# The last batch's attention output made turned, in 512 columns, in place of rows

## Chip, core and metric

One core of one Trainium2 chip runs one program: linear attention, then two feed-forward blocks. The metric is device time in microseconds (us), the median of the runs. TensorE (PE) does matmuls into eight PSUM banks, VectorE (DVE) and ScalarE (ACT) read PSUM, GpSimd (POOL) works between SBUF tiles, and SyncE (SP) issues the DMAs. Every engine runs its own instructions in the order in which the program holds them; semaphores make one wait for another.

## Reference, cut to what matters

```python
# attention: batch 4, heads 8, sequence 576, head size D 64, features M 128
q_p, k_p = phi(q_s), phi(k_s)
kv = np.einsum('bhsm,bhsd->bhmd', k_p, v)
z = np.sum(k_p, axis=2)
num = np.einsum('bhsm,bhmd->bhsd', q_p, kv)
den = np.einsum('bhsm,bhm->bhs', q_p, z)[..., None] + 1e-06
x = num / den                      # 2304 tokens x 512
# first block: 512 -> 2048 -> 512
h = np.maximum(x @ w_in, 0.0); x = h * h @ w_out
# second block: rms norm, gate and value 512 -> 1536 -> 512
```

`phi` is an exponential of a projection, less its norm and its maximum. All is in fp32. Where the kernel wants fast matmuls on fp32 data it splits an operand in two fp32r parts, high and low, and adds three products (high by high, high by low, low by high).

## The kernel before

The sequence of each batch is cut into 512 tokens (128 partitions times R = 4 rows) and a rest of 64 (SR). The four batches' 512 tokens are four blocks of the first feed-forward, `moe1(0)` to `moe1(3)`; the rests of all four batches make a fifth, `moe1(REM)`. `moe1(j)` runs over 16 chunks of 128 hidden columns: `hpart(c)` (12 matmuls of 512 columns into a bank `h`, L845) and `ypart(c)` (12 into four banks `acc`, L875). Then `moe2` does the second block, twice two batches (L1081, L1142).

The attention of batch b + 1 is woven into the matmuls of `moe1(b)`. `attention(b)` takes the eight heads as four pairs. For a pair: features of k and q (L604, exponentials on ACT at L628), `kv2` (L671, L674: key features times values and a column of ones, into one bank `kvp`; L658 also turns the rest's q features there), then the output. That is, in the long form which the last two batches use:

- `trs` (L726): eight 128x128 transposes of the q features into two banks; `copy` takes them to `qt` (ACT or DVE).
- `mms` (L731, L735): the turned q features are the weights, and `kv` with its column z (65 columns) is what moves: eight fp32 matmuls, and two for the rest. The output lies in rows, each with its denominator beside it.
- `rows` (L703 to L707): on DVE, the denominators of four rows plus epsilon, their reciprocal (4 columns), and the quotient.
- `xtr` (L773, L763): the finished rows are turned back by four transposes of 128 columns and one of 64, and `split` (L403 on ACT, L394 on DVE) makes the high and low part of `x`, which `hpart` of `moe1(b + 1)` reads.

Past the first batch all this goes through the two banks `t`. A fp32 matmul of `mms` or `kv2` shows in the trace as two TensorE instructions.

The order of every engine's instructions is set when the kernel is built, by `Plan`: a list scheduler that walks a clock of its own with an assumed cost of each piece, and at each step takes the ready piece of the least `prio` whose buffers are free. The priorities of a pair are `pb` (the batch's base, plus 3.7 for each pair) plus some tenths of its step. What the planner put in order stays in that order on the chip, however long the pieces take there. Weights for `moe1` come from HBM through a ring of 8 buffers `wr`. Between these, DVE and ACT decode weights for the second block (`decode`, L432 to L446), off TensorE's path.

Of the kernel before, what the change touches and what calls it, by code (L numbers as in the profile page):

```python
# [247 lines left out]
def kernel(  # L248
# [23 lines left out]
    nc = tc.nc  # L272
# [28 lines left out]
    slots = {  # L301
# [5 lines left out]
    }  # L307
    plan = Plan(slots)
# [60 lines left out]
    def f32(t):  # L369
        return t.bitcast(F32)  # L370
# [11 lines left out]
    def pe(n, cnt, passes=1):  # L382
        return cnt * passes * max(0.109, 0.0133 + n / 2400.0)
# [151 lines left out]
    def attention(b):  # L535
        base = (b - 1) * float(C1) if b else -25.0
        step = 3.7 if b else 6.0
        lead = base - (6.0 if b else 3.95)
        full, long = b < FULL, b >= LONG
        rem_x = []  # L540
        ssr = Buf(["sm"])

# [19 lines left out]
        def rem_prep(pr0):  # L562
# [3 lines left out]
            row_norms(pr0, xr, ssr)  # L566
            dma(lead, lambda: vr_t[P - SR:], lambda: rest_v[b], 133120, w=[b_vr])

        def pair(hp):
            banks = ["t"] if b else ["t", "h", "acc"] if hp < 3 else ["t", "acc"]  # L570
            pb = base + hp * step
            h0 = 2 * hp
            bv = b_v[(b * HP + hp) % 2]
            vt = v_t[(b * HP + hp) % 2]
# [79 lines left out]
            qrt = Buf(["qr"])  # L654

            def qtr2(o):
                for h in range(2):
# [21 lines left out]
                    plan.add("PE", 0.224 * 5, pb + 3 * u + h * u, kv, [(pk, h * R), pr, bv, b_vr, b_vz], [(kvp, h)],  # L679
                             kv_free)  # L680
            if long:
                plan.add("PE", 0.224 * 10 + 0.27, pb + 4 * u, kv2, [pk, pr, bv, b_vr, b_vz, b_const], [kvp], kv_free,
                         pre=[qrt])
# [115 lines left out]
    def moe1(j):  # L799
# [172 lines left out]
    def read_units(c, pos, gates):  # L972
        return {nm: read_unit(c, nm, pos + {"g": 0.0, "v": 0.3, "s": 0.05, "o": 1.0}[nm[0]], gates) for nm in UNITS}
# [61 lines left out]
    def operands(j, rv, p0, cls, gates, room):  # L1035

        ops = {nm: [] for nm in ("B11", "T2", "B21", "T3", "T1", "T4", "B22")}
        for kk in range(2):
# [12 lines left out]
            minus(p + 0.05, t, b22, t, 512)  # L1051
            two("T2", t, p + 0.05)
            two("T3", b12, p + 0.1)
            two("B22", b22, p + 0.1)
            b21 = scaled(p + 0.1, j, kk + 2, rv[0], gates, room)
            minus(p + 0.1, t, b21, t, 512)
            gates = [plan.nodes[-1]]
            two("B21", b21, p + 0.1)
            two("T4", t, p + 0.1)
        return ops  # L1060

    def operands_rem(rv, p0, gates, room):
        ops = {"B1": [], "B2": [], "D": []}
        for kk in range(2):
# [254 lines left out]
```

## Time and profile before

| what | us |
|---|---|
| three runs, median (lowest to highest) | 1006.02 (1003.1 to 1006.41) |
| the profiled execution, its own time | 1006.28 |
| its span in the trace | 1004.5 |
| PE busy in the span | 989.2 |
| DVE busy | 712.2 |
| ACT busy | 525.6 |
| mean granted TensorE clock | 0.996 of full |

Between span and time lie 1.8 us. A busy PE is one with a matmul in its pipe; how long a group of matmuls takes is read better from its start to the start of the next group. The page's chain of work that ended last lies for 88% of the span on PE.

### The profile page before, as it was taken

What the parts mean: (1) busy time and instruction counts of PE and PEld (TensorE: products, weight loads), DVE (VectorE), ACT (ScalarE), POOL (GpSimd) and SP (SyncE); (2) the same over time, 40 slices, a digit from 0 to 9 for tenths busy, and PEclk for the clock granted to TensorE, in tenths of its full rate; (3) what the DMA queues carried; (4) which work ended last, traced back from release to release, by engine and by line L of the source; (5) the groups of instructions that cost most, each with busy time, mean ns of one, the idle gap of its engine ahead of it and who ended that gap; (6) DMA issues with size and microseconds to landing.
All of it is one profiled execution on the core that took longest, in us unless ns stands there. A gap on an engine that the chain in (4) does not pass through costs nothing.

```text
span 1004.5 us, 14617 instructions
## 1 busy us (share of the span) xinstructions
PE 989.2 (98%) x5140; PEld 838.4 (83%) x5140; DVE 712.2 (71%) x1374; ACT 525.6 (52%) x1097; POOL 122.3 (12%) x101
## 2 busy tenths in 40 slices
PE   8999999999999999999999999999998999999998
PEld 7888888888888888888789978888886888888887
DVE  5989998577658576655622879889797747576673
ACT  5878888545564555544534557654353444224220
POOL 0110132131110101100000302311043000000000
PEclk9999999999999999999999999999999999999999
DMA  7777888976667575678868435234243212212213
GB/s 244 255 243 251 280 263 307 303 256 228 242 216 260 188 247 185 226 255 286 281 216 267 146 106 162 80 116 137 75 123 108 83 53 63 74 31 79 71 32 104
DMA packets 74841, 179.36 MB, mean 179 GB/s; under 512 B 8848, under 2 KB 12048, under 8 KB 74768
## 3 DMA queue, kind: packets, MB, share of 16 engines
q1 hardware_dynamic: 74768, 178.43, 54.2%
q8 instruction: 40, 0.66, 0.3%
q14 instruction: 33, 0.27, 0.1%
HBM read 143.27 MB, written 35.13 MB: 178 GB/s over the span
## 4 chain that ended last, share of the span: by engine, by line
PE 88%; DVE 4%; DMA 4%; issue 1%; ACT 1%; POOL 1%; SPq 0%; ACTq 0%; POOLq 0%; DVEq 0%
PE acc L875 18%; PE h L845 18%; PE acc L1081 11%; PE t L1142 11%; PE h L1081 10%; PE t L1081 3%; PE t L731 3%; PE t L604 2%; PE t L601 2%; PE t L671 2%; DMA st<-y 2%; PE t L726 1%; PE h L1142 1%; DVE cc L1101 1%; DVE wq L394 1%
## 5 line engine op out<-in xcount | busy, mean ns | idle before, releaser
L875 PE MATMUL acc<-g,wr 128*128 128x512 f32 (+1 forms) x660 | 151.7, 374 | 0.7 <-DVE g L394 0.7
L845 PE MATMUL h<-x,wr 128*128 128x512 f32 x528 | 133.4, 396 | 0.0
L875 PEld LDWEIGHTS acc<-g,wr 128*128 128x128 f32 x660 | 113.6, 189 | 21.3 <-DVE g L394 1.5
L1142 PE MATMUL t<-wq,ub 128*128 128x512 f32 x462 | 114.5, 392 | 0.7 <-DVE oa L1150 0.7
L1081 PE MATMUL acc<-x,wq 128*128 128x512 f32 x321 | 111.5, 396 | 1.8 <-DVE f L894 1.8
L845 PEld LDWEIGHTS h<-x,wr 128*128 128x128 f32 x528 | 97.2, 188 | 19.2
L403 ACT CAST wq<-wq 128x512 fp32r<-128x512 f32 x108 | 66.3, 619 | 87.3 <-DMA wq<-w2d4g 14.8
L1142 PEld LDWEIGHTS t<-wq,ub 128*128 128x128 f32 x462 | 86.7, 189 | 20.6 <-DVE oa L1150 2.4
L394 DVE TENSOR_TENSOR g<-f,g 128x512 fp32r<-128x512 f32 (+1 forms) x67 | 46.4, 693 | 70.1 <-ACT f L515 58.8
L859 ACT ACTIVATE f<-h 128x512 f32<-128x512 f32 (+1 forms) x80 | 44.9, 562 | 92.4 <-PE h L845 86.1
L1081 PE MATMUL acc<-xa,wq 128*128 128x512 f32 x231 | 89.9, 396 | 3.1 <-ACT xa L403 3.1
L394 DVE TENSOR_TENSOR wq<-wq 128x512 fp32r<-128x512 f32 x99 | 74.1, 756 | 25.5 <-ACT wq L403 25.0
L1081 PE MATMUL h<-x,wq 128*128 128x512 f32 x255 | 81.0, 390 | 0.0
L1081 PEld LDWEIGHTS acc<-x,wq 128*128 128x128 f32 x321 | 61.1, 191 | 15.1 <-DVE f L894 2.3
L875 PE MATMUL acc<-g,wu 128*128 128x512 f32 (+1 forms) x300 | 70.7, 376 | 0.2 <-DVE g L394 0.2
L1081 PE MATMUL h<-xa,wq 128*128 128x512 f32 x201 | 69.3, 390 | 0.4 <-DVE xa L394 0.4
L628 ACT ACTIVATE p<-t,sm 128x128 f32<-128x128 f32 x216 | 60.0, 383 | 18.1 <-DVE sm L619 18.1
L1101 DVE TENSOR_TENSOR cc<-acc,cc 128x512 f32<-128x512 f32 x84 | 57.7, 686 | 14.8 <-PE acc L1081 13.8
L1150 DVE TENSOR_TENSOR oa<-t,oa 128x512 f32<-128x512 f32 x75 | 50.8, 686 | 23.1 <-PE t L1142 22.7
L845 PE MATMUL h<-x,wu 128*128 128x512 f32 x240 | 61.6, 398 | 0.0
L875 PEld LDWEIGHTS acc<-g,wu 128*128 128x128 f32 x300 | 51.5, 189 | 9.5 <-DVE g L394 0.8
L441 ACT ACTIVATE dw<-st 128x512 f32<-128x512 f32 x68 | 46.6, 696 | 22.8 <-DMA st<-in_w_out_dram 9.4
(245 smaller groups left out, 1818.8 us busy)
## 6 DMA issues: line engine op xcount, KB each, us to landing
wr<-w1d SPq DMA_DIRECT2D x88, 512.0 KB, 4.3
st<-in_w_out_dram SPq DMA_DIRECT2D x28, 512.0 KB, 4.7
w1d<-wr SPq DMA_DIRECT2D x22, 512.0 KB, 4.1
st<-in_w_in_dram SPq DMA_DIRECT2D x16, 512.0 KB, 4.5
st<-in_w_gate_dram SPq DMA_DIRECT2D x12, 512.0 KB, 5.9
st<-in_w_val_dram SPq DMA_DIRECT2D x12, 512.0 KB, 5.9
st<-y SPq DMA_DIRECT2D x23, 256.0 KB, 4.1
v<-in_v_r_dram SPq DMA_DIRECT2D x16, 260.0 KB, 3.2
```

Source lines behind the costliest of these rows:

```text
L394: return lambda: en.tensor_tensor(out=lo(), in0=src(), in1=f32(hi()), op=ALU.subtract)
L403: first = plan.add("ACT", act(n), prio, lambda: nc.scalar.copy(out=hi(), in_=src()), rd, [whi], after, pre=[blo] if blo is not bhi else [])
L441: lambda: nc.scalar.activation(out=out(), in_=hf(), func=AF.Abs, scale=65536.0), [(st, 1)], [w])
L628: nc.scalar.activation(out=pbuf.ap[:, j0 + i, :], in_=fp.ap[:, i, :], func=AF.Exp, bias=mx.ap[:, i:i + 1])
L731: nc.tensor.matmul(np.ap[:, r * D1:(r + 1) * D1], lhsT=qt.ap[:, r * P:(r + 1) * P], rhs=kvt[:, h, :], start=True, stop=True)
L845: nc.tensor.matmul(hb.ap[:, :n], lhsT=u.ap[:, wl, kk * P:(kk + 1) * P], rhs=xcols(j, xl, kk)(), start=(gi == 0 and ii == 0), stop=(gi == l ...
L859: lambda: nc.scalar.activation(out=rb.ap[:, :n], in_=hb.ap[:, :n], func=AF.Relu), [hb], [rb])
L875: nc.tensor.matmul(accs[e].ap[:, :n], lhsT=u.ap[:, w, es], rhs=x.ap[:, :n], start=(c == 0 and i == 0), stop=(c == C1 - 1 and i == 2))
L1081: nc.tensor.matmul(bank.ap[:, cols], lhsT=u.ap[:, wl, c0 + kk * P:c0 + (kk + 1) * P], rhs=x[kk][xl].ap[:, :cols.stop - cols.start], start= ...
L1101: lambda: nc.vector.tensor_tensor(out=out.ap, in0=bank.ap, in1=x.ap, op=ALU.add), [bank, x], [out])
L1142: nc.tensor.matmul(o.ap, lhsT=x[xl].ap[:, c0:c0 + P], rhs=us[f"o{i}"].ap[:, wl, :], start=i == n == 0, stop=i == 1 and n == 2)
L1150: lambda: nc.vector.tensor_tensor(out=oa.ap, in0=o.ap, in1=oa.ap, op=ALU.add), [o, oa], [oa])
```

## The change

It touches the last batch (`turn = b == B - 1`), the planner's inputs around it, and two numbers of buffers.

- `turned_pair` takes the place of `mms`, `rows` and `xtr` for the four pairs of batch 3. From `kvp` it makes a weight tile of 256 columns, in a high and a low part: for each head 64 columns of kv and 64 copies of z (`k_hi` on ACT, `k_lo` on DVE). The rest's turned q features are split as well. `rest` is then six fp32r matmuls of 64 columns, `mms` six of 512 columns with q's turned features as what moves; these are now split in two (ACT and DVE) where they were copied. The result is turned already: 64 partitions of numerators and 64 of denominators, the denominators 64 times alike.
- `quotient` divides: ACT brings denominators (plus epsilon) and numerators to the right halves of the partitions, 64 partitions by 512 columns four times (and by 64 columns four times for the rest), DVE takes the reciprocal of all 128x512 denominators in two halves and multiplies. The product is split from SBUF.
- The ring `wr` goes from 8 to 7 buffers and `xw` from 2 to 3. The pairs of batch 3 have `pb` lower by 1.0.
- `moe1(REM)`'s `hpart` comes after the last `hpart` of batch 3; loads for the norms and the units of `moe2`, and its scaled operands, wait for further nodes.

```diff
@@ turned_pair, new
+            plan.add("ACT", 0.4, p0, k_hi, [kvp], [(k2, 0)])
+            plan.add("DVE", 0.4, p0, k_lo, [kvp, (k2, 0)], [(k2, 1)])
...
+            split(pb + 5 * u, qr_, lambda: qrh.ap, lambda: qrl.ap, 2 * SR, [kvp], qrh, qrl, psum=True)
+            er = Buf(banks, view=lambda t: t[:, :2 * SR].rearrange("p (h n) -> p h n", h=2))
+            PARTS = ((0, 0), (0, 1), (1, 0))
+            def product(o, h, x):
+                for i, (wl, xl) in enumerate(PARTS):
+                    nc.tensor.matmul(o, lhsT=k2.ap[:, wl, h * P:(h + 1) * P], rhs=x[xl](), start=i == 0, stop=i == 2)
...
+            plan.add("PE", 6 * 0.06, pb + 5.5 * u, rest, [k2, qrh, qrl], [er])
+            qps = [Buf(banks), Buf(banks)]
...
+            plan.add("PE", 0.88, pb + 6 * u, trs, [pq, b_const], qps)
+            for h in range(2):
+                split(pb + 6.2 * u, lambda h=h: qps[h].ap, lambda h=h: qh[h].ap, lambda h=h: ql[h].ap, 512, [qps[h]],
+                      qh[h], ql[h], psum=True)
+            nps = [Buf(banks), Buf(banks)]
...
+            plan.add("PE", 6 * 0.2267, pb + 8 * u, mms, [k2, *qh, *ql], nps)
@@ quotient
+                    nc.scalar.activation(out=xf.ap[lo_, cs], in_=den[0](hi_), func=AF.Copy, bias=EPS_DEN)
+                    nc.scalar.activation(out=xf.ap[hi_, cs], in_=den[1](lo_), func=AF.Copy, bias=EPS_DEN)
...
+                    return lambda: nc.vector.reciprocal(out=xf.ap[:, c0:c1], in_=xf.ap[:, c0:c1])
...
+                    nc.scalar.copy(out=nm.ap[lo_, :n], in_=num[0](lo_))
+                    nc.scalar.copy(out=nm.ap[hi_, :n], in_=num[1](hi_))
...
+                         lambda: nc.vector.tensor_tensor(out=xf.ap[:, cs], in0=nm.ap[:, :n], in1=xf.ap[:, cs], op=ALU.mult),
...
@@ attention, pair, moe1, moe2
-        "xr": 4, "wu": 10, "wr": 8, "dw": 2,
+        "xr": 4, "wu": 10, "wr": 7, "dw": 2,
-            pb = base + hp * step
+            pb = base + hp * step - (1.0 if b == 3 else 0.0)
+                if turn:
+                    turned_pair(pb, u, b, hp, pq, kvp, qrt, banks)
+                    return
...
-                h_nodes[c] = plan.add("PE", pe(n, len(group)), base + c, mm, list(dict.fromkeys(wb + xb)), [hb])
+                h_nodes[c] = plan.add("PE", pe(n, len(group)), base + c, mm, list(dict.fromkeys(wb + xb)), [hb],
+                                      [h_all[B - 1, C1 - 1]] if j == REM else [])
...
-    sets = [read_units(c, E1 + (c - 1.0 if c else -7.0), []) for c in range(NC2)]
+    sets = [read_units(c, E1 + (c - 1.0 if c else -7.0), [rv.users[0] for rv in rv01]) for c in range(NC2)]
```

The place that the prediction turns on is the passage from `moe1(2)` to `moe1(3)`, where the fourth pair's `x` is first read. In the rows, `acc` are the output banks of `moe1`, `h` a hidden bank, `t` the attention's banks, `g` the hidden activations, `x` the attention's output; the numbers name buffers. On PE before, from the turning back of the fourth pair to the first chunk of `moe1(3)`:

```order
L773 MATMUL t_4999<-ident,xw_4954 128x128 x4
L763 MATMUL t_5000<-ident,xw_4954 128x64
L875 MATMUL acc_3819<-g_4899,wr_4539 128x512
...
L875 MATMUL acc_3838<-g_4899,wr_4539 128x512
L845 MATMUL h_5032<-x_4037,wr_4665 128x512
L845 MATMUL h_5032<-x_4355,wr_4665 128x512
L845 MATMUL h_5032<-x_4745,wr_4665 128x512
L845 MATMUL h_5032<-x_5001,wr_4665 128x512
```

Nine `acc` matmuls of batch 2 stand between the turning back and the chunk, and its fourth matmul is the first to read the fourth pair's `x` (`x_5001`). On PE now, the same stretch, from the last `acc` matmul of batch 2:

```order
L981 MATMUL acc_3835<-g_4925,wr_4580 128x512
L601 MATMUL t_5012<-qr_4971,xw_4993 128x64
...
L615 MATMUL t_5034<-ident,p_4912 128x128 x4
L615 MATMUL t_5035<-ident,p_4912 128x128 x4
L601 MATMUL t_5067<-qt_5049,xw_4993 128x512
...
L601 MATMUL t_5068<-qt_5055,xw_4993 128x512
L950 MATMUL h_5098<-x_4139,wr_4666 128x512
L950 MATMUL h_5098<-x_4510,wr_4666 128x512
L950 MATMUL h_5098<-x_4831,wr_4666 128x512
L950 MATMUL h_5098<-x_5094,wr_4666 128x512
```

The last `acc` matmul has moved ahead of the fourth pair's whole output: `rest`, `trs` and `mms` follow each other with no other matmul between them, and the chunk that reads `x_5094` comes straight behind. On DVE before, the fourth pair's rows and its split (`sm` are the denominators of four rows):

```order
L707 TENSOR_TENSOR xw_4954<-t_4952,sm_4977 128x4x64
L706 RECIPROCAL sm_4977<-sm_4977 64x2
L703 TENSOR_SCALAR sm_4977<-t_4953 128x4
L707 TENSOR_TENSOR xw_4954<-t_4952,sm_4977 64x128
L706 RECIPROCAL sm_4977<-sm_4977 128x4
L707 TENSOR_TENSOR xw_4954<-t_4953,sm_4977 128x4x64
...
L394 TENSOR_TENSOR x_5002<-t_4999,x_5001 128x512
L432 TENSOR_SCALAR st_5021<-st_5021 128x512
```

No decoding step stands between the quotients and the low part of `x`; the next one (`st_5021`) comes behind it. On DVE now, over the same stretch (`st`, `dw` belong to the decoding of the second block's weights, `ld` is the low part of q's turned features):

```order
L1000 COPY f_5009<-acc_3826 128x512
L432 TENSOR_SCALAR st_4986<-st_4986 128x512
...
L641 RECIPROCAL xw_5026<-xw_5026 128x64
...
L437 TENSOR_SCALAR st_4991<-st_4991 128x512
L394 TENSOR_TENSOR ld_5050<-t_5034,qt_5049 128x512
L446 SCALAR_TENSOR_TENSOR dw_5045<-dw_5045,st_4991 128x512
L394 TENSOR_TENSOR ld_5056<-t_5035,qt_5055 128x512
...
L641 RECIPROCAL xw_5026<-xw_5026 128x256 x2
L655 TENSOR_TENSOR xw_5026<-ld_5086,xw_5026 128x512
L394 TENSOR_TENSOR x_5095<-xw_5026,x_5094 128x512
```

Two decodings of four steps each (`st_4986`, `st_4991`) now stand ahead of and between the two low parts, and the two reciprocals of 256 columns ahead of the product.

## Rows read from the trace of the kernel before

**Rows 1.** The page: busy time, share of the span and instructions of each engine.

```profile
PE 989.2 (98%) x5140; PEld 838.4 (83%) x5140; DVE 712.2 (71%) x1374; ACT 525.6 (52%) x1097; POOL 122.3 (12%) x101
```

**Rows 2.** Whom PE waited for: total us, times, longest us.

```profile
PE acc L1081 <- ACT xa L403: 3.1, 1, 3.1
PE acc L1081 <- DVE f L894: 1.8, 1, 1.8
```

**Rows 3.** PE in order of time, fourth pair: start, us, line, out<-in, shape, count.

```profile
429.83 1.00 PE L731 MATMUL t<-kv,qt 128*128 128x65 f32 x8
430.76 0.45 PE L735 MATMUL t<-kv,qr 128*64 128x65 f32 x4
431.13 1.11 PE L731 MATMUL t<-kv,qt 128*128 128x65 f32 x8
432.05 2.10 PE L845 MATMUL h<-x,wr 128*128 128x512 f32 x8
...
434.68 0.60 PE L773 MATMUL t<-ident,xw 128*128 128x128 f32 x4
435.21 0.27 PE L763 MATMUL t<-ident,xw 64*128 64x64 f32 x1
435.41 2.33 PE L875 MATMUL acc<-g,wr 128*128 128x512 f32 x9
437.58 2.88 PE L845 MATMUL h<-x,wr 128*128 128x512 f32 x12
440.30 2.88 PE L875 MATMUL acc<-g,wr 128*128 128x512 f32 x12
```

**Rows 4.** PE in order of time, a little earlier: fp32r of 256 columns, and transposes.

```profile
417.05 0.28 PE L604 MATMUL t<-bd_hi,tt 128*128 128x256 f32 x1
417.17 0.28 PE L604 MATMUL t<-bd_lo,tt 128*128 128x256 f32 x1
...
426.64 1.03 PE L726 MATMUL t<-ident,p 128*128 128x128 f32 x8
427.44 1.64 PE L875 MATMUL acc<-g,wu 128*128 128x512 f32 x6
```

**Rows 5.** ACT in order of time, fourth pair; in brackets idle time and its releaser.

```profile
425.41 0.66 ACT L441 ACTIVATE dw<-st 128x512 f32<-128x512 f32 x1
425.98 0.25 ACT L509 COPY qr<-t 128x128 f32<-128x128 f32 x1
427.28 1.08 ACT L509 COPY qt<-t 128x512 f32<-128x512 f32 x2 [1.05 <-PE t L726]
...
435.52 0.21 ACT L403 CAST xr<-t 128x64 fp32r<-128x64 f32 x1
```

**Rows 6.** DVE in order of time, fourth pair.

```profile
426.71 0.42 DVE L432 TENSOR_SCALAR st<-st 128x512 uint32<-128x512 uint32 x1
427.05 0.68 DVE L446 SCALAR_TENSOR_TENSOR dw<-dw,st 128x512 uint32<-128x512 uint32 x1
427.65 0.74 DVE L437 TENSOR_SCALAR st<-st 128x512 uint16<-128x512 uint16 x1
428.18 0.46 DVE L443 TENSOR_SCALAR dw<-dw 128x512 f32<-128x512 f32 x1
...
436.22 0.68 DVE L394 TENSOR_TENSOR g<-f,g 128x512 fp32r<-128x512 f32 x1
436.82 0.68 DVE L394 TENSOR_TENSOR x<-t,x 128x512 fp32r<-128x512 f32 x1
```

**Rows 7.** DVE in order of time, the norms ahead of the second block.

```profile
549.57 4.98 DVE L1011 RECIPROCAL wq<-wq 128x256 f32<-128x256 f32 x3 [1.57 <-ACT wq L1007]
```

**Rows 8.** Stretches: length, busy us of each engine (instructions), granted clock, DMA.

```profile
580.00:583.30 3.30, 1.04 (x5) 0.52 (x4) 3.30 (x7) 1.65 (x3) 0.00 (x0) 1.00 0.31 81
583.30:587.20 3.90, 3.90 (x11) 3.06 (x12) 2.14 (x4) 2.66 (x4) 0.00 (x0) 0.59 0.23 71
...
425.00:450.00 25.00, 25.00 (x126) 20.82 (x127) 15.69 (x34) 10.43 (x20) 1.51 (x1) 1.00 0.69 242
```

More of the change, by code (lines that the diff above doesn't have):

```diff
@@ L538, in attention @@
         lead = base - (6.0 if b else 3.95)
-        full, long = b < FULL, b >= LONG
+        full, long, turn = b < FULL, b >= LONG, b == B - 1
         rem_x = []
@@ L567, in rem_prep, with turned_pair, at, k_hi @@
             dma(lead, lambda: vr_t[P - SR:], lambda: rest_v[b], 133120, w=[b_vr])
+        def turned_pair(pb, u, b, hp, pq, kvp, qrh, banks):
+            k2 = Buf(["xw"], view=lambda t: t.rearrange("p r n -> p (r n)")[:, :512].bitcast(F32R).rearrange(
+                "p (a n) -> p a n", a=2))
+            qrl = Buf(["qr"], view=lambda t: t.bitcast(F32R))
+            kv_ = lambda: kvp.ap[:, :2, :D]
+            z_ = lambda: kvp.ap[:, :2, D:D + 1].to_broadcast([P, 2, D])
+            def at(i, q):
+                return k2.ap[:, i, :].rearrange("p (q d) -> p q d", d=D)[:, q, :]
+            KV, Z = slice(0, 4, 3), slice(1, 3)
+            def k_hi():
+                nc.scalar.copy(out=at(0, KV), in_=kv_())
+                nc.scalar.copy(out=at(0, Z), in_=z_())
+            def k_lo():
+                nc.vector.tensor_tensor(out=at(1, KV), in0=kv_(), in1=f32(at(0, KV)), op=ALU.subtract)
+                nc.vector.tensor_tensor(out=at(1, Z), in0=z_(), in1=f32(at(0, Z)), op=ALU.subtract)
+            p0 = pb + 4.5 * u
+            plan.add("ACT", 0.4, p0, k_hi, [kvp], [(k2, 0)])
+            plan.add("DVE", 0.4, p0, k_lo, [kvp, (k2, 0)], [(k2, 1)])
+            qr_ = lambda: kvp.ap[:, 2, :].rearrange("p (h n) -> p h n", h=2)
+            split(pb + 5 * u, qr_, lambda: qrh.ap, lambda: qrl.ap, 2 * SR, [kvp], qrh, qrl, psum=True)
[4 more added lines that the diff above has]
+                    nc.tensor.matmul(o, lhsT=k2.ap[:, wl, h * P:(h + 1) * P], rhs=x[xl](), start=i == 0, stop=i == 2)
+            def rest():
+                for h in range(2):
+                    product(er.ap[:, h, :], h, [lambda h=h: qrh.ap[:, h, :], lambda h=h: qrl.ap[:, h, :]])
+            plan.add("PE", 6 * 0.06, pb + 5.5 * u, rest, [k2, qrh, qrl], [er])
+            qps = [Buf(banks), Buf(banks)]
+            qh = [Buf(["qt"], view=lambda t: t.bitcast(F32R)) for _ in range(2)]
+            ql = [Buf(["ld"], view=lambda t: t.rearrange("p h r d -> p (h r d)").bitcast(F32R)) for _ in range(2)]
+            def trs():
+                for h in range(2):
+                    for r in range(R):
+                        nc.tensor.transpose(qps[h].ap[:, r * P:(r + 1) * P], pq.ap[:, h * R + r, :], ident)
+            plan.add("PE", 0.88, pb + 6 * u, trs, [pq, b_const], qps)
+            for h in range(2):
+                split(pb + 6.2 * u, lambda h=h: qps[h].ap, lambda h=h: qh[h].ap, lambda h=h: ql[h].ap, 512, [qps[h]],
+                      qh[h], ql[h], psum=True)
+            nps = [Buf(banks), Buf(banks)]
+            def mms():
+                for h in range(2):
+                    product(nps[h].ap, h, [lambda h=h: qh[h].ap, lambda h=h: ql[h].ap])
+            plan.add("PE", 6 * 0.2267, pb + 8 * u, mms, [k2, *qh, *ql], nps)
+            xf = Buf(["xw"], view=lambda t: t.rearrange("p r n -> p (r n)"))
+            rest_c, main_c = slice(512, 512 + SR), slice(0, 512)
+            def quotient(p1, num, den, cs, rd):
+                lo_, hi_ = slice(0, D), slice(D, 2 * D)
+                n = cs.stop - cs.start
+                def dens():
+                    nc.scalar.activation(out=xf.ap[lo_, cs], in_=den[0](hi_), func=AF.Copy, bias=EPS_DEN)
+                    nc.scalar.activation(out=xf.ap[hi_, cs], in_=den[1](lo_), func=AF.Copy, bias=EPS_DEN)
+                def recip(c0, c1):
+                    return lambda: nc.vector.reciprocal(out=xf.ap[:, c0:c1], in_=xf.ap[:, c0:c1])
+                nm = Buf(["ld"], view=lambda t: t.rearrange("p h r d -> p (h r d)"))
+                def nums():
+                    nc.scalar.copy(out=nm.ap[lo_, :n], in_=num[0](lo_))
+                    nc.scalar.copy(out=nm.ap[hi_, :n], in_=num[1](hi_))
+                plan.add("ACT", 2 * act(n), p1, dens, rd, [(xf, cs.start)])
+                plan.add("ACT", 2 * act(n), p1, nums, rd, [nm])
+                for c0 in range(cs.start, cs.stop, 256):
+                    c1 = min(c0 + 256, cs.stop)
+                    plan.add("DVE", 0.1 + (c1 - c0) * 0.0064, p1, recip(c0, c1), [(xf, cs.start)], [(xf, cs.start)])
+                plan.add("DVE", Shared(dve(n)), p1,
+                         lambda: nc.vector.tensor_tensor(out=xf.ap[:, cs], in0=nm.ap[:, :n], in1=xf.ap[:, cs], op=ALU.mult),
+                         [nm, (xf, cs.start)], [(xf, cs.start)])
+            for hl in range(2):
+                b_x[b, hl, hp] = Buf(["x"])
+            xh, xl = b_x[b, 0, hp], b_x[b, 1, hp]
+            rh, rl = b_xr[0, hp // 2], b_xr[1, hp // 2]
+            cr = slice(b * SR, (b + 1) * SR)
+            ers = [lambda ps, h=h: er.ap[ps, h, :] for h in range(2)]
+            quotient(pb + 7 * u, ers, ers, rest_c, [er])
+            split(pb + 8.6 * u, lambda: xf.ap[:, rest_c], lambda: rh.ap[:, hp % 2, cr], lambda: rl.ap[:, hp % 2, cr], SR,
+                  [(xf, 512)], (rh, (b, hp)), (rl, (b, hp)))
+            ns = [lambda ps, h=h: nps[h].ap[ps, :] for h in range(2)]
+            quotient(pb + 8.5 * u, ns, ns, main_c, nps)
+            split(pb + 9.5 * u, lambda: xf.ap[:, main_c], lambda: xh.ap, lambda: xl.ap, 512, [(xf, 0)], xh, xl)
@@ L653, in pair @@
             kv_free = list(bkv.users)
-            qrt = Buf(["qr"])
+            qrt = Buf(["qr"], view=lambda t: t.bitcast(F32R)) if turn else Buf(["qr"])
             def qtr2(o):
@@ L681, in pair @@
             if long:
-                plan.add("PE", 0.224 * 10 + 0.27, pb + 4 * u, kv2, [pk, pr, bv, b_vr, b_vz, b_const], [kvp], kv_free,
-                         pre=[qrt])
+                plan.add("PE", 0.224 * 10 + 0.27, pb + 4 * u, kv2, [pk, pr, bv, b_vr, b_vz, b_const], [kvp],
+                         [] if turn else kv_free, pre=[qrt])
+                if turn:
+                    turned_pair(pb, u, b, hp, pq, kvp, qrt, banks)
+                    return
                 copy(pb + 6.2 * u, lambda: qrt.ap, lambda: kvp.ap[:, 2, :].rearrange("p (h n) -> p h n", h=2), 2 * SR,
@@ L1037, in operands @@
         ops = {nm: [] for nm in ("B11", "T2", "B21", "T3", "T1", "T4", "B22")}
+        gates = gates + [r.users[-1] for r in rv]
         for kk in range(2):
@@ L1063, in operands_rem @@
         ops = {"B1": [], "B2": [], "D": []}
+        gates = gates + rv.users[-1:]
         for kk in range(2):
@@ L1232 @@
     room = ["st", "dw"]
-    rv01 = [rms(j, E1 - 10.0, [h3[4 + 2 * j]], ["xa"], room, ["wq"]) for j in range(2)]
+    rv01 = [rms(j, E1 - 10.0, [h3[4 + 2 * j], *last[-2:]], ["xa"], room, ["wq"]) for j in range(2)]
     x01 = operands(0, rv01, E1 - 8.0, ["x", "xa"], [h3[9]], room)
```

2 rows, old and new, of the table slots are left out of this document.

## The prediction

> **What bounds the kernel now.** I read the page's busy times first: PE is busy 98% of the span, DVE 71%, ACT 52% [rows 1]. Then the list of what PE waited for: nine entries, of which the two longest are 3.1 and 1.8 us, both in the second block [rows 2], and none in the attention of the last batch. Then PE in order of time through the last batch's fourth pair: each group starts where the one ahead has issued its last matmul, and the first chunk of `moe1(3)` follows at 437.58 without a gap [rows 3]. So this stretch costs what PE's instructions take from start to start, and work on DVE and ACT costs nothing as long as its results come in time. From 425 to 450 DVE is busy 15.69 of 25 us and ACT 10.43 [rows 8]: they have room on the average. The reader should ask two things of the change: how much PE work goes, and whether what PE now needs of DVE and ACT still lies beside other matmuls.
>
> **PE work removed.** `mms` runs from 429.83 to 432.05, that is 2.22 us; `xtr` from 434.68 to 435.41, 0.73 us [rows 3]. Together 2.95 us a pair.
>
> **PE work added.** Six fp32r matmuls of 512 columns: twelve take 440.30 - 437.58 = 2.72 us [rows 3], so six take 1.36. Six of 64 columns (`rest`): the trace has no fp32r matmul so narrow. Above, 256 columns take 0.12 [rows 4], and a 65-column pass of `mms` 0.93 / 8 = 0.116, the rest's 0.37 / 4 = 0.093 [rows 3]. Below, half of a 128-column transpose of 0.80 / 8 = 0.10 [rows 4], 0.05. I take 0.10, since all narrow matmuls here lie at 0.09 to 0.12 whatever their columns: 0.6 us, between 0.3 and 0.7. Net 2.95 - 1.36 - 0.60 = 0.99 a pair (0.87 to 1.29), and for four pairs **-4.0 us** (-5.2 to -3.5). `kv2`, `trs` and the features stay.
>
> The Trainium skill (TensorE: Matmul & The Clock Gate, "Back-to-back issue gap") gives matmuls of up to 64 columns an issue gap of some 60 cycles, about 25 ns, when nothing else binds. By it the four `rest` groups would take an estimated 0.6 us in all, and the sum would be 1.8 us lower than by my 0.10; no narrow matmul of this trace comes near it, so the rows keep the price.
>
> **The other engines' work.** Per pair DVE loses the row quotients (some 1.9 us of small steps) and gains the low parts of kv and of two 512-column q tiles, two reciprocals of 256 columns, one of 64, and a product. A DVE step of 512 columns starts 0.6 us after the one ahead [rows 6]; three reciprocals of 256 took 4.98 us [rows 7], 1.66 each. That makes about 7 us in place of 2.7, +4.5 a pair, 18 in all. ACT gains four copies of 64 partitions by 512. The trace has no ACT step on 64 partitions; I price it as 128x512, 1.08 / 2 = 0.54 [rows 5], the row of the same width; half of it, for half of the elements, is the other bound. For the first three pairs I let this lie beside `moe1(2)`: in the order each has at least 3 us of matmuls between `trs` and `mms`, and `h` and `acc` chunks behind `mms`. What is left of DVE's room there is a third of a pair's time at most, and banks `t` are held longer, so later features can wait. I allow 0 to 4 us for that and take 1.0. The ring of 7, the moved loads and the gates I cost at nothing: PE waited for no `wr` load before, and its order in the second block is the same; if a gate made one load late there, the wait would look like the 3.1 of [rows 2].
>
> **The fourth pair stands open.** This is where the change costs. Before, nine `acc` matmuls (2.17 us from 435.41 to 437.58) lay over the cast of the fourth pair's `x` [rows 3]. Now the last `acc` matmul of batch 2 stands ahead of `rest`, and from there to the chunk that reads the fourth `x` PE has only `rest` (0.6), `trs` (0.8), `mms` (1.36) and three matmuls of the chunk (0.68): 3.44 us. Beside it runs a chain that must go its whole length. I walk it from T = 0 at the end of the last `acc` matmul, with 0.2 us for each handing over (transposes of a half issue until about 427.04, the copy starts at 427.28 [rows 4, 5]), ACT steps of 512 columns at 0.54, 64-column ones at 0.2 (0.21), a decoding step of ACT at 0.57 [rows 5], and on DVE L432 0.34, L446 0.60, L437 0.53, L443 0.5 [rows 6]:
>
> - ACT copies the last `acc` bank (0.2 to 0.75), decodes (to 1.35), takes the rest's two denominators and two numerators (to 2.1). Only then is the second bank free, so the second half of `trs` runs from 2.3 to 2.7.
> - ACT decodes again (to 2.7), casts q's two halves (to 3.25 and 3.8). DVE works through its order: `acc` copy (to 0.6), L432, L437, L443, the 64-column reciprocal (about 0.45), L446, L432, L443 (behind ACT), L437, to 4.5. Then the first low part (to 5.1), L446 (to 5.7), the second low part (to 6.3).
> - `mms`: the first three start at 5.35, the other three at 6.5 and end at 7.2.
> - ACT's denominators to 8.0, its numerators to 9.1. DVE's two reciprocals from 8.2 to 11.5, the product to 12.2, ACT's cast from 12.4 to 13.0.
> - PE's fourth matmul of the chunk starts at 13.2.
>
> So PE stands still 13.2 - 3.44 = **9.8 us**. If DVE had its decoding done in advance and ACT too, the same walk gives: `trs` done at 2.15, low parts at 3.7, `mms` at 4.6, denominators at 5.4, reciprocals at 8.9, cast at 10.3, PE at 10.4, a stall of 7.0. With half price for 64 partitions it is 6.2. I take 9.8: the loads of these weights run ahead in SP's order, but in DVE's order the two decodings come behind the `acc` copy, which itself waits for PE, so they can't be done early. A late load there would make it more, 2 us at most I guess from a decoding's four steps (1.97).
>
> **The clock.** After the idle time before 583.3, PE's granted clock was 0.59 of full for 3.9 us and was 1.00 before it [rows 8]; that is mostly the lower level, 1.2 GHz. It cost 3.9 x 0.41 = 1.6 us. The stall here is longer, so I add 1.6 behind it, and 0.3 for the last matmuls of `mms` inside it (none to 0.6).
>
> **Sum.** -4.0 + 9.8 + 1.6 + 0.3 + 1.0 = +8.7. Against the profiled execution's 1006.28 that is 1015.0; the median of the runs lies 0.26 lower, so **1014.7 us**. Bounds of the terms: -5.2 + 6.2 + 1.6 = +2.6 gives 1008.6; -3.5 + 9.8 + 2.0 + 1.6 + 0.6 + 4.0 = +14.5 gives 1020.5.
>
> **Rivals.**
> 1. The saving shows whole: the fourth pair's chain would have to be hidden, as it was. 1006.0 - 4.0 = 1002.0. For it: PE hardly waits anywhere now. Against it: no matmul stands in PE's order that could hide it, and the chain's reciprocals alone take 3.3. Chance 0.04.
> 2. The stall is short and something is given back: the lower bound of 7.0 plus 1.6 of clock, and the 1.8 wait at the second block's entry goes (with its 1.6 of clock), since loads and `acc` copies stand otherwise there: -4.0 + 8.6 - 3.4 = +1.2, about 1007.2, within 0.3%. Against it: PE's order at that entry and the number of DVE steps ahead of the last `acc` copy are as before. Chance 0.08.
> 3. DVE becomes the bound through `moe1(2)` too: with +4.5 us a pair its low parts of `g` come late for `acc`. If each pair's added work overran the room by 1.5 to 2 us, 6 to 8 us would come on top: 1021. It decides from the point at which DVE's idle share in that stretch goes to nothing; 63% busy speaks against it. Chance 0.10.
>
> **Chances.** The forecast 0.78. A measurement here can tell about 0.3% (3.0 us) from no change. Faster 0.04, within 0.08, slower 0.88. The forecast's own bounds are 1008.6 to 1020.5; I take the low end to 1007.0 so that rival 2 lies inside. Outside are rivals 1 and 3, 0.14.
>
> **What would show it.** After: `rest` and `mms` of a pair together near 2.0 us, no `xtr`. In the list of what PE waited for, a wait of `mms` for DVE's low parts (2 to 4 us) and one of `h` at the chunk for ACT's cast of `x` (4 to 6 us), and a granted clock well under 1 for about 4 us behind it. If PE's timeline goes through this passage without those two, the prediction is wrong, and so it is if the first three pairs show waits of more than 4 us together.

## The result

| kernel | runs | median (lowest to highest), us |
|---|---|---|
| before | 4 | 1006.21 (1003.1 to 1007.34) |
| after | 4 | 1016.62 (1013.0 to 1018.88) |

The ratio is 1.0108, with a 95% interval of 1.0084 to 1.0132: the change makes the kernel about 10 us slower. The forecast was 1014.7 in a range of 1007.0 to 1020.5. The profiled execution of after took 1013.0 us and is the fastest of its four; its span is 1011.2.

### The profile page after: what moved, and what is told of

It reads as the page before. It is cut to its first block, busy times and chain, and to the rows that moved or that the text cites. A ratio compares the mean times of both kernels' runs of the same rounds, so it can differ in the third digit from the quotient of the medians.

```text
span 1011.2 us, 14550 instructions
## 1 busy us (share of the span) xinstructions
PE 986.6 (98%) x5088; PEld 834.3 (83%) x5088; DVE 725.3 (72%) x1366; ACT 544.5 (54%) x1141; POOL 127.8 (13%) x105
## 4 chain that ended last, share of the span: by engine, by line
PE 88%; DVE 7%; ACT 2%; DMA 2%; issue 1%; SPq 0%; POOL 0%; DVEq 0%; POOLq 0%; ACTq 0%
PE h L950 19%; PE acc L981 18%; PE t L1250 11%; PE acc L1189 11%; PE h L1189 10%; PE t L1189 3%; PE t L706 2%; PE t L703 2%; PE t L836 2%; PE t L773 2%; PE h L1250 1%; DVE wq L394 1%; PE t L831 1%; DVE cc L1209 1%; DVE xw L641 1%
## 5 line engine op out<-in xcount | busy, mean ns | idle before, releaser
L981 PE MATMUL acc<-g,wr 128*128 128x512 f32 (+1 forms) x660 | 151.0, 373 | 0.6 <-DVE g L394 0.4
L950 PE MATMUL h<-x,wr 128*128 128x512 f32 x528 | 135.5, 400 | 4.2 <-ACT x L403 4.2
L981 PEld LDWEIGHTS acc<-g,wr 128*128 128x128 f32 x660 | 113.8, 189 | 21.3 <-DVE g L394 1.2
L950 PEld LDWEIGHTS h<-x,wr 128*128 128x128 f32 x528 | 98.7, 191 | 24.9 <-ACT x L403 5.0
L1189 PE MATMUL acc<-x,wq 128*128 128x512 f32 x321 | 110.5, 393 | 0.0
L1189 PE MATMUL acc<-xa,wq 128*128 128x512 f32 x231 | 89.0, 393 | 3.6 <-ACT xa L403 3.2
L1189 PE MATMUL h<-x,wq 128*128 128x512 f32 x255 | 81.6, 392 | 0.6 <-DVE x L394 0.6
L1189 PE MATMUL h<-xa,wq 128*128 128x512 f32 x201 | 69.9, 393 | 2.7 <-ACT xa L403 1.9
L1189 PEld LDWEIGHTS acc<-x,wq 128*128 128x128 f32 x321 | 61.1, 190 | 13.1 <-DVE cc L1209 0.4
L981 PE MATMUL acc<-g,wu 128*128 128x512 f32 (+1 forms) x300 | 70.2, 375 | 0.0
L1209 DVE TENSOR_TENSOR cc<-acc,cc 128x512 f32<-128x512 f32 x84 | 57.7, 687 | 13.9 <-PE acc L1189 11.3
L950 PE MATMUL h<-x,wu 128*128 128x512 f32 x240 | 61.6, 397 | 0.0
L981 PEld LDWEIGHTS acc<-g,wu 128*128 128x128 f32 x300 | 51.6, 189 | 8.9
L1189 PEld LDWEIGHTS h<-x,wq 128*128 128x128 f32 x255 | 47.6, 189 | 10.8 <-DVE x L394 1.0
```

What stands on the lines that cost most here:

```text
L981: nc.tensor.matmul(accs[e].ap[:, :n], lhsT=u.ap[:, w, es], rhs=x.ap[:, :n], start=(c == 0 and i == 0), stop=(c == C1 - 1 and i == 2))
L1189: nc.tensor.matmul(bank.ap[:, cols], lhsT=u.ap[:, wl, c0 + kk * P:c0 + (kk + 1) * P], rhs=x[kk][xl].ap[:, :cols.stop - cols.start], start= ...
L1209: lambda: nc.vector.tensor_tensor(out=out.ap, in0=bank.ap, in1=x.ap, op=ALU.add), [bank, x], [out])
```

## The profile after

Line numbers of the code behind `turned_pair` are about 105 higher than before: `hpart` is L950, `ypart` L981, the second block's products L1189; `rest` and `mms` share L601, `trs` is L615. The page's line of busy times answers [rows 1]:

```profile
PE 986.6 (98%) x5088; PEld 834.3 (83%) x5088; DVE 725.3 (72%) x1366; ACT 544.5 (54%) x1141; POOL 127.8 (13%) x105
```

PE is busy for 2.6 us less and the span is 6.7 us longer. The list of what PE waited for (total, times, longest; sorted by total, parts left out):

```profile
PE h L950 <- ACT x L403: 4.2, 1, 4.2
PE acc L1189 <- ACT xa L403: 3.2, 1, 3.2
PE t L601 <- DVE ld L394: 2.1, 2, 1.8
PE h L1189 <- ACT xa L403: 1.9, 1, 1.9
...
PE t L615 <- ACT ld L647: 1.1, 1, 1.1
...
PE h L1189 <- DVE xa L394: 0.8, 1, 0.8
PE h L1189 <- DVE x L394: 0.6, 1, 0.6
```

The second stands in [rows 2] too, with 3.1. The first, third and fifth of these lines have no like there; they are one place, the fourth pair. PE in order of time there, from the last `acc` matmuls of batch 2 on (start, us, line, operation, shape, count; in brackets idle time and its releaser):

```profile
429.30 2.35 PE L981 MATMUL acc<-g,wr 128*128 128x512 f32 x9
431.49 0.76 PE L601 MATMUL t<-qr,xw 128*128 128x64 f32 x6
432.08 0.66 PE L615 MATMUL t<-ident,p 128*128 128x128 f32 x4
433.83 0.66 PE L615 MATMUL t<-ident,p 128*128 128x128 f32 x4 [1.10 <-ACT ld L647]
436.33 0.50 PE L601 MATMUL t<-qt,xw 128*128 128x512 f32 x1 [1.84 <-DVE ld L394]
...
437.53 0.79 PE L601 MATMUL t<-qt,xw 128*128 128x512 f32 x1 [0.24 <-DVE ld L394]
...
438.98 1.48 PE L950 MATMUL h<-x,wr 128*128 128x512 f32 x3
444.70 3.73 PE L950 MATMUL h<-x,wr 128*128 128x512 f32 x9 [4.24 <-ACT x L403]
448.26 2.88 PE L950 MATMUL h<-x,wu 128*128 128x512 f32 x12
```

Before, the chunk of `moe1(3)` followed the pair without a gap [rows 3]. Now 16.77 us pass from the start of `rest` at 431.49 to the second chunk at 448.26, for work that takes 5.48 at full speed (the prediction's 3.44, and 2.04 for nine more matmuls). So the passage costs 11.3 us. The four bracketed waits add up to only 7.4 of it: most of the rest is slow matmuls in and behind the stall. The windows view gives the nine matmuls behind it (length, busy us by engine, granted clock):

```profile
444.70:448.26 3.56, 3.56 (x9) 2.88 (x10) 2.70 (x5) 0.53 (x1) 0.00 (x0) 0.57 0.00 0
```

DVE in the same stretch shows the chain and what stands in it:

```profile
431.61 0.42 DVE L432 TENSOR_SCALAR st<-st 128x512 uint32<-128x512 uint32 x1
432.06 0.75 DVE L437 TENSOR_SCALAR st<-st 128x512 uint16<-128x512 uint16 x1
...
436.20 0.68 DVE L446 SCALAR_TENSOR_TENSOR dw<-dw,st 128x512 uint32<-128x512 uint32 x1
436.79 0.68 DVE L394 TENSOR_TENSOR ld<-t,qt 128x512 fp32r<-128x512 f32 x1
...
439.84 3.36 DVE L641 RECIPROCAL xw<-xw 128x256 f32<-128x256 f32 x2 [0.71 <-ACT xw L638]
443.30 0.69 DVE L655 TENSOR_TENSOR xw<-ld,xw 128x512 f32<-128x512 f32 x1
```

Decoding (L432 to L446) comes ahead of q's low part, then two reciprocals take 3.36 us, and only then come the product and the cast for which `h` waits.

To place the rest I read three points in each kernel's timeline of PE: the first matmul of `mms` for the fourth pair of batch 1 (`kv` is what moves; long ahead of the changed pairs), the first matmul of the second block, and the end. The first stretch is free of what the start of the program happened to cost (the first point is at 167.68 before, at 165.61 after):

| kernel | first point to second block | second block |
|---|---|---|
| before | 408.7 | 428.1 |
| after | 415.1 (+6.4) | 430.5 (+2.4) |

Sum: 6.4 + 2.4 - 2.1 (the earlier first point) = 6.7, the difference of the spans. Over all traces of this document the first point lies between 164.5 and 167.8, turned pairs or not.

## The experiments

The same three points for every experiment, in us (each from its one profiled execution), with the ratio of its runs to those of the kernel before on the same chip. The profiled execution is not always a typical one: e11's took 1015.83 us and is the slowest of twelve with a median of 1007.96, e7's took 1018.28 and is the slowest of six with a median of 1014.63. Their stretches can't be compared with the others to a us.

| run | pairs turned | to second block | second block | ratio (95%) |
|---|---|---|---|---|
| e1_first_three | 1 to 3 | 411.4 | 428.6 | 1.0036 (1.0022 to 1.0051) |
| e3_sides_only | none | 408.6 | 430.7 | 1.0017 (1.0001 to 1.0033) |
| e4_earlier3 | all | 424.9 | 429.4 | 1.0200 (1.0170 to 1.0231) |
| e6_three_earlier3 | 1 to 3 | 420.2 | 427.9 | 1.0112 (1.0091 to 1.0134) |
| c_short_recip | all | 413.0 | 432.5 | 1.0096 (1.0074 to 1.0118) |
| e7_decode_yields | all | 415.9 | 435.3 | 1.0109 (1.0090 to 1.0128) |
| e8_rows_decode_yields | none | 416.2 | 425.5 | 1.0052 (1.0036 to 1.0068) |
| e9_rows_no_gates | none | 408.2 | 428.5 | 1.0003 (0.9990 to 1.0016) |
| e10_yield_42 | all | 404.3 | 431.0 | 0.9985 (0.9967 to 1.0003) |
| e11_yield_40 | all | 413.8 | 432.5 | 1.0033 (1.0013 to 1.0053) |
| e12_rows_yield_42 | none | 409.3 | 431.7 | 1.0038 (1.0023 to 1.0052) |
| e13_yield_41_ring8 | all | 403.4 | 432.3 | 0.9989 (0.9970 to 1.0007) |

Theory: the loss is the turned fourth pair's chain, which nothing covers. Rivals: turned pairs overload DVE wherever they stand; the edits beside them (ring, priorities, gates) make the loss; the late place alone does.

### Which part of the change: e3, e1

All pairs in rows, everything else kept:

```diff
-        full, long, turn = b < FULL, b >= LONG, b == B - 1
+        full, long, turn = b < FULL, b >= LONG, False
```

> All four pairs in rows as before; only the other edits stay (ring wr 7, three xw buffers, last batch's priorities earlier by 1.0, the added gates). Theory: these cost what the second block's entry lost in the changed kernel, 0 to 2.2 us, and no wait stands in the passage from moe1(2) to moe1(3): 1006 to 1008.5. Rival (the other edits, not the turned pairs, make the loss): 1013 or more.

1006.71 us. No wait in the passage; the first stretch is as before (408.6 against 408.7), the second block 2.6 longer. The other edits are not the loss: 1.0017 here, 1.0108 for the whole change.

Three pairs turned, the fourth in rows:

```diff
+            turn = b == B - 1 and hp < 3
             pb = base + hp * step - (1.0 if b == 3 else 0.0)
```

> Pairs one to three of the last batch are made turned, the fourth in rows as before; all other edits stay. In PE's order the fourth pair still stands last in batch 2: six acc matmuls between its trs and mms, nothing between mms and xtr, nothing between xtr and the first chunk of moe1(3). Theory (the loss is the length of the turned fourth pair's chain, where nothing covers it): the stall of 9.8 us and the 1.5 us of slow clock go, 3.0 us of PE work are saved, the rows' shorter chain (quotient about 2 us, cast 0.6) leaves 2 to 3 us of stall, and the second block's entry still costs some 2 more: 1006 - 3.0 + 2.5 + 2 = about 1008 (1005 to 1010). Rival (it is the late place alone that costs, whatever form the pair has): PE still waits over 7 us in the passage, 1013 or more. Rival (the turned form costs in all pairs): 1013 or more with no long wait in the passage.

1008.64 us, as the theory had it, but by other terms: the second block costs 0.5 more than before instead of some 2, and the stall is 4.7 us instead of 2 to 3 (PE's list of waits; here lines behind the edit are one higher):

```profile
PE t L879 <- DVE xw L813: 4.7, 1, 4.7
```

DVE's timeline says why. The quotient of the rows takes DVE steps of 0.14 to 0.42 us, but the planner put decoding between them:

```profile
433.65 0.74 DVE L437 TENSOR_SCALAR st<-st 128x512 uint16<-128x512 uint16 x1
434.17 0.47 DVE L443 TENSOR_SCALAR dw<-dw 128x512 f32<-128x512 f32 x1
434.54 0.16 DVE L809 TENSOR_SCALAR sm<-t 128x4 f32<-128x4 f32 x1
434.67 0.69 DVE L446 SCALAR_TENSOR_TENSOR dw<-dw,st 128x512 uint32<-128x512 uint32 x1
435.28 0.17 DVE L812 RECIPROCAL sm<-sm 128x4 f32<-128x4 f32 x1
...
437.91 0.42 DVE L813 TENSOR_TENSOR xw<-t,sm 128x256 f32<-128x256 f32 x1
```

So the late place costs in either form, and the turned form costs more there: 11.3 us in all, against 4.7 and 1.5 of slow clock (the twelve matmuls behind took 4.25 us, 439.80 to 444.05, in place of 2.72). So rows in that place lose 6.2, over half of the 11.3. Why the fourth pair stands so late here and not in e3, where acc and h matmuls stand between its steps, no run shows.

### What the stall consists of: c_short_recip

```diff
+                    c1 = c0 + 4 if hp == 3 else c1
                     return lambda: nc.vector.reciprocal(out=xf.ap[:, c0:c1], in_=xf.ap[:, c0:c1])
```

> The changed kernel, but the fourth pair's three reciprocals take only 4 columns each instead of 256, 256 and 64, so the rest of that pair's denominators stays undivided; the order of every engine stays. Theory (the stall is the chain, and the reciprocals are a part of it until something else in the chain is later): the two large reciprocals take some 0.3 us in place of 3.36, but ACT's second copy of numerators ends at 441.0, so the product can start at 441.2 instead of 443.3 and the fourth matmul of the chunk follows 11.1 us after the start of rest in place of 13.2: 2.1 us less, 1016.5 - 2.1 = about 1014.4. If the reciprocals alone set the end, it is 3.1 less (1013.4). Rival (the wait is for something outside the pair's chain): no change, 1016 to 1017.

From the start of `rest` to the fourth matmul of the chunk 10.8 us (433.88 to 444.68) in place of 13.2. DVE's rows show the end that was foreseen: behind the short reciprocals the product waits for ACT's numerators. The last two rows are PE's.

```profile
442.09 0.24 DVE L642 RECIPROCAL xw<-xw 128x4 f32<-128x4 f32 x2 [0.71 <-ACT xw L638]
443.29 0.69 DVE L656 TENSOR_TENSOR xw<-ld,xw 128x512 f32<-128x512 f32 x1 [0.95 <-ACT ld L648]
...
444.68 2.35 PE L951 MATMUL h<-x,wr 128*128 128x512 f32 x9 [1.97 <-ACT x L403]
446.87 2.89 PE L951 MATMUL h<-x,wu 128*128 128x512 f32 x12
```

The nine matmuls behind took 2.19 us at a granted clock of 1.00, after an idle time of 1.97 us in place of 4.24. The length of the idle time alone does not decide this: at the second block's entry before, matmuls behind a wait of 1.8 us [rows 2] ran at 0.59 [rows 8]. To the second block it is 2.1 shorter than after, not the whole 3.8 that the passage gained (last section): this execution has three waits elsewhere (0.35, 0.30 and 0.74 us) that after's has not. The whole times (1014.1, ratio 1.0096 against 1.0108) agree with a small gain but could not show it alone. So 3.1 us of reciprocals are worth 2.4 of stall; without them the chain is still 10.8 long. The fourth pair's denominators stay undivided in this kernel, so it serves only for this measurement.

### Covering the chain by an earlier pair: e4, e6

```diff
-            pb = base + hp * step - (1.0 if b == 3 else 0.0)
+            pb = base + hp * step - (3.0 if b == 3 else 0.0)
```

> All four pairs turned; the last batch's priorities are earlier by 3.0 in place of 1.0, which puts four h and twelve acc matmuls (3.6 us) between the fourth pair's trs and mms and twelve acc matmuls (2.7 us) between its mms and the first chunk of moe1(3). Theory (the chain is as long as before, the cover decides): of the 6.0 us from the end of mms to the cast of x 3.4 are covered, so PE waits 2.6 us there and little ahead of mms; the clock may still fall for 1.5. 1006 - 4.0 + 2.6 + 1.5 + 2 = about 1008 (1005 to 1010). Rival (DVE cannot keep up with the added work, wherever PE's matmuls stand): the waits move, the time stays at 1013 to 1019.

In the passage the theory holds: `mms` starts without a wait, and PE waits 3.4 us for `x` (forecast 2.6). But the time is 1025.84, because another hole opens 120 us earlier, ahead of `moe1(2)`:

```profile
PE t L878 <- ACT p L730: 8.1, 1, 8.1
PE h L950 <- ACT x L403: 3.4, 1, 3.4
```

Batch 3's first pair now stands between the last transposes of batch 2 and the matmuls that would have covered them. In DVE's queue the first of its statistics (L717) is done at 314.4, but the next (L721) stands behind a decoding step that waits 2.49 us for its load, and behind the rest of two decodings; ACT's exponentials and PE stand behind L721:

```profile
313.75 0.69 DVE L717 TENSOR_REDUCE sm<-t 128x4 f32<-128x512 f32 x1 [0.59 <-PE t L706]
316.93 0.43 DVE L432 TENSOR_SCALAR st<-st 128x512 uint32<-128x512 uint32 x1 [2.49 <-DMA st<-in_w_val_dram]
...
320.43 0.15 DVE L721 SCALAR_TENSOR_TENSOR sm<-sm,sm 128x4 f32<-128x4 f32 x1
```

The same with the fourth pair in rows:

> Pairs one to three turned, the fourth in rows, and the last batch's priorities earlier by 3.0: twelve h and twelve acc matmuls now stand between the fourth pair's mms and its xtr, and nine acc matmuls (with four h) behind it ahead of the chunk that reads it. Theory: no wait in the passage, 3.0 us of PE work saved, the second block's entry costs 0 to 2.2 more: 1003 to 1005.5. Rival (three turned pairs cost on DVE or at the banks t what they save on PE): 1006 or more, with waits of t, g or x in the passage.

1016.2 us, missed for the same reason: the same wait ahead of `moe1(2)` (8.0 us), none in the passage. Moving whole pairs earlier moves the hole.

### Covering it by decoding that yields: e7, e8

Both times decoding stood in front of a step that PE needed. Its priority `pos` is ahead of the pairs'; now it is put behind:

```diff
-            decode(pos, st, lambda: w.ap, w)
+            decode(max(pos, 54.0), st, lambda: w.ap, w)
```

(and likewise for the four `both_sbuf` steps of `make_halves`).

> All four pairs turned, and the second block's decoding steps (decode and the sums and differences of its halves) get a priority behind the last batch's attention instead of ahead of it. In the new order eight DVE steps of decoding no longer stand in the fourth pair's chain, and PE has a chunk of h and fifteen acc matmuls (6.1 us) between the fourth mms and moe1(3). Theory (the loss was the uncovered chain, lengthened by decoding ahead of hot steps): no long wait in the passage, PE's saving of 4.0 shows, the second block's entry still costs 0 to 2.5: 1006 - 4.0 + 1.5 = about 1003.5 (1002 to 1005). Rival (turned pairs overload DVE, which then is late elsewhere): 1008 or more with new waits for DVE in moe1(2). Rival (the decoded weights now come late for the second block): 1008 or more with waits for wq at its entry.

The passage is as the theory wants it: from `rest` to the first chunk of `moe1(3)` at 436.08 PE waits once, 0.66 us, and for `g`, not for the pair:

```profile
425.54 0.76 PE L601 MATMUL t<-qr,xw 128*128 128x64 f32 x6
...
428.99 2.91 PE L950 MATMUL h<-x,wr 128*128 128x512 f32 x12
431.74 3.11 PE L981 MATMUL acc<-g,wr 128*128 128x512 f32 x13
435.51 0.73 PE L981 MATMUL acc<-g,wr 128*128 128x512 f32 x2 [0.66 <-DVE g L394]
436.08 2.89 PE L950 MATMUL h<-x,wr 128*128 128x512 f32 x12
```

Yet the time is 1014.63: the gain is given back in `moe1(REM)` and at the second block's entry, and the forecast of 1003.5 missed.

```profile
PE h L1190 <- ACT x L403: 6.4, 1, 6.4
PE acc L981 <- POOL g L394: 3.8, 1, 3.8
```

By the code, the added gate `last[-2:]` makes the second block's norms wait for the last decoded halves, which now come late; no run took this gate alone away.

> All four pairs in rows, with all other edits of the change and the same later priority of the decoding as in the run beside it. Theory: PE already went through the passage without a wait, so the later decoding gives nothing here: as with the other edits alone, 1006 to 1007.5; the difference from the turned kernel beside it is then the price of turning, 2 to 4 us in its favour. Rival (the later decoding itself is what gains): this kernel is as fast as the turned one beside it, within 1 us.

Missed too: 1009.3 us, with a wait of 4.3 us for `g` in `moe1(REM)` that the forecast had not. Against e3, which has rows and the same other edits, the later decoding alone costs 0.0035 of the time here, some 3.5 us (1.0052 and 1.0017). So the loss of the run beside it is at least in part decoding put off too far, not turning.

### The right amount: e10, e11, e12, e13

Decoding at 42 or later, and the norms' gate undone:

```diff
-            decode(pos, st, lambda: w.ap, w)
+            decode(max(pos, 42.0), st, lambda: w.ap, w)
...
-    rv01 = [rms(j, E1 - 10.0, [h3[4 + 2 * j], *last[-2:]], ["xa"], room, ["wq"]) for j in range(2)]
+    rv01 = [rms(j, E1 - 10.0, [h3[4 + 2 * j]], ["xa"], room, ["wq"]) for j in range(2)]
```

> All four pairs turned; decoding gets a priority of at least 42 instead of 54 (so it is put off less), and the rms steps of the second block no longer wait for the last decoded halves' stores. In the new order 14 matmuls of h and acc stand between the fourth pair's trs and mms, and 39 (8.9 us) between its mms and moe1(3). Theory (the loss is the uncovered chain, and what the run before lost again was decoding put off too far, by which the second block's rms came late): no long wait in the passage, entry waits of the second block as in the changed kernel, 3 to 4 us: 4.0 less for PE's work, 0 to 2 more at the entry, so 2 to 4 us below the kernel before. Rival (any putting off of decoding gives the gain back): waits of 4 us or more in moe1(REM) or at the entry, 3 us or more above the kernel before.

1004.56 us, 0.9985 of before (0.9967 to 1.0003): some 12 us better than after. The first stretch is 4.4 us shorter than before. The fourth pair in PE's timeline:

```profile
422.08 0.75 PE L601 MATMUL t<-qr,xw 128*128 128x64 f32 x6
422.66 1.63 PE L981 MATMUL acc<-g,wu 128*128 128x512 f32 x6
424.13 0.39 PE L601 MATMUL t<-qt,xw 128*128 128x512 f32 x1
...
425.53 1.53 PE L981 MATMUL acc<-g,wu 128*128 128x512 f32 x6
```

`mms` follows its cover without a wait. The lower priority does two things at once: it takes decoding out of the chain and it changes PE's order, so that other matmuls stand beside the chain; these runs don't part the two, nor the gate undone here from the priority. The second block takes back 2.9 us, so the forecast of 2 to 4 below before came out as about 1.5, which is not told from no change.

> As the run beside it with a priority of decoding of at least 40. In the new order 27 matmuls of h and acc stand between the fourth pair's trs and mms and 18 (4.1 us) between its mms and moe1(3). Theory: of the chain's 6.0 us from the end of mms to the cast of x 4.8 are covered, PE waits 1.2 us there; decoding is put off least: 1 to 3 us below the kernel before. Rival (any putting off of decoding gives the gain back): waits of 4 us or more in moe1(REM) or at the entry, 3 us or more above the kernel before.

1007.96 us, slower than before by 1.0033. The profiled execution took 1015.83, the slowest of twelve, so what it shows need not stand in the others. In it PE waited 1.8 us for `x` (forecast 1.2), and behind it a decoding step on DVE and ACT stood waiting for its load ahead of `moe1(3)`'s own steps; PE waited 1.9 and 1.3 us more, and eleven `acc` matmuls behind took 4.2 us at a granted clock of 0.59, where they take 2.5 at full speed. Why the typical execution is slower than before stays open.

```profile
445.86 0.43 DVE L432 TENSOR_SCALAR st<-st 128x512 uint32<-128x512 uint32 x1 [3.73 <-DMA st<-in_w_val_dram]
```

The price of turning by itself, with e10's priorities and rows:

> The same priorities and gates as in the run e10_yield_42, with all four pairs in rows: the two differ only in how the last batch's output is made. Theory (turned pairs save 0.99 us of PE work each, and this shows whole once nothing waits in the passage): 4.0 us above e10_yield_42, that is 3 to 4 us above the kernel before, with no more waits of PE than there. Rival (the later decoding is what brought the time down, turning gives nothing): within 1 us of e10_yield_42, equal to the kernel before.

1009.05 us, 1.0038. The two differ by 0.0053 of the time, 5.3 us (some 3 to 8 by the two intervals), and their first stretches by 4.9 (409.3 and 404.3). Turning gains what was forecast, 4.0; whether it gains more is not told. What e12 loses against before lies mostly in the second block, 3.6 us.

> As e10_yield_42 with decoding at 41, the ring wr back at 8 buffers and xw at two; PE's order around the fourth pair has the same cover. Theory (ring and xw cost nothing, what is left is the gates at the second block's entry): within 1 us of e10_yield_42, 0 to 2 us below the kernel before. Rival (the smaller ring costs time): 1.5 us or more below e10_yield_42.

1003.04 us, 0.9989 (0.9970 to 1.0007): not told from e10. The ring of 7 and the third `xw` cost nothing that can be measured, if decoding at 41 does as at 42, which this run changes too. No version here is faster than before by more than a measurement tells.

### The gates: e9

> All four pairs in rows, ring of 7, three xw buffers and the earlier priorities kept, all five added gates taken away. Theory (the gates, which make the second block's loads later, cost what the other edits lost): its entry's waits go back to those of before, 2.3 us in place of 3.3, and the time to that of before, 1005 to 1006. Rival (the ring of 7 or the earlier priorities cost it): 1006.5 to 1007.5, with the entry's waits at 3.3 us.

1004.68 us, 1.0003, and a second block of 428.5 against e3's 430.7. The ratio's interval overlaps e3's, and its entry's waits are 3.0 us, not 2.3. The gates are the likely price in e3, not a shown one: e1 and e6 have all the gates and a second block of 428.6 and 427.9. Which order at that entry is dear was not settled. No run has turned pairs without the gates.

## The prediction, step by step

- **PE work removed and added: right.** Over four pairs, from start to next start, `rest` took 2.34 us and `mms` 5.57 in e10, where `mms` and `xtr` had taken 8.88 and 2.92 before: 3.9 us saved, forecast 4.0. `rest` takes 0.59 us a pair (431.49 to 432.08), 0.098 a matmul: the 0.10 from neighbouring rows. The issue gap of some 25 ns that the prediction quoted from the Trainium skill (TensorE: Matmul & The Clock Gate, "Back-to-back issue gap") is not met by these matmuls, at 98 ns each.
- **The walk of the fourth pair: right.** Forecast: `mms` at 5.35 and 6.5, reciprocals at 8.2, the fourth matmul at 13.2 us. Measured from 431.49: 4.84, 6.04, 8.35 and 13.21. That the end fits to 0.01 us is luck: `mms` started 0.5 sooner than forecast, and its second three matmuls took 1.45 us in place of 0.7. The stall is 13.21 - 3.44 = 9.8. That decoding stands in the chain was right as well, and e1 shows that it delays the short rows too.
- **ACT on 64 partitions: right.** L637 to L647 took 0.58 to 0.59 us for 64x512, the price of 128x512, not half of it. The prediction said that the trace before has no ACT step on 64 partitions; it has two, at the start (L498, 64x128, 0.31 us each, where the copy of 128x128 in [rows 5] takes 0.25), and they spoke against half price.
- **DVE's added work: 13.1 us more busy time (725.3 against 712.2), forecast 18.** 7 in place of 2.7 us is 4.3 a pair, too, not 4.5. The reciprocals of the four pairs alone take 16.0 us; DVE has less of other work, which the forecast did not consider. No term of the sum is worked out from it.
- **The clock: right, one part counted twice.** Behind the stall 3.56 us in place of 2.04, 1.5 more (forecast 1.6), at a granted clock of 0.57 ([rows 8] had 0.59), so mostly at the lower level of 1.2 GHz. The 0.3 for `mms` inside the stall does not come on top: it lies inside the 13.2.
- **Waits of the other pairs: mis-sized.** The forecast added 1.0 (0 to 4). There is no such wait in PE's list, and what is left of the first stretch is 6.4 - 11.3 + 3.9 = -1.0. This and the 0.9 by which e12 and e10 differ beyond the 4.0 were not traced to an instruction.
- **The second block's entry: missed.** Ring, gates and moved loads were costed at nothing. After took 2.4 us more in the second block, e3 with rows 2.6; waits of 0.6, 1.9 and 0.8 us in after's list stand where before had 0.4 and 1.8. The prediction said that such a wait would look like [rows 2]; it gave it no price.
- **The rivals.** (1) and (2) fall with the stall. (3), DVE as the bound through `moe1(2)`, falls: PE waits for nothing in the first three pairs, and e10, with the same turned pairs, is 12 us faster.

So the sum for the profiled execution was 1015.0 against 1013.0: the passage 0.4 too dear, the other pairs 2.0 too dear, the second block 2.4 too cheap, and 2.1 from the start of the program, which no term could hold. The passage, which carries the forecast, is right in mechanism and size; that the total came so near is in part luck, since the other misses, of 2.0 to 2.4 us each, don't all have the same sign. The median lies 3.6 above that execution, and so 1.9 above the forecast; where the other executions lose could not be read, since only this one has a trace.

## What to carry to other kernels

A cheaper piece on the bounding engine is worth its saving only if its longer chain on other engines keeps cover: before counting matmuls, list what stands between the last producer and the first consumer at a stage's end. The same four pairs cost 10 us here or nothing, by the order around them. Background work that is "off the path" sits in the same in-order queues, so look for it ahead of the hot steps in a stall, and when moving it or the hot steps, look at the next hole that this opens.

## What the hardware showed beyond that

- A fp32 reciprocal of 128x256 on DVE took 1.68 us (3.36 for two), where a subtraction of 128x512 took 0.68: five times as long a column. The Trainium skill (VectorE: DVE Perf Modes, "First, the fixed hardware budget") has the reciprocal as an iterative divide with a repeat count of 8; in this trace a column takes 4.9 times the subtraction's time.
- An ACT copy of 64 partitions took as long as one of 128 (0.58 us for 512 columns).
- The chain's shortening by 2.4 us saved 3.8 in the passage (16.77 to 12.99 us from `rest` to the second chunk), since the nine matmuls behind it ran at full clock. In the stall itself the second three matmuls of after's `mms` took 1.45 us (437.53 to 438.98), where three take 0.68 at full speed.
